# Rationing the clock-keeping matmuls of TensorE by an account kept over all steps instead of one per step

## The chip, the cores and the metric

The kernel runs on one core of one Trainium2 chip. The metric is the device time of one execution in microseconds (us), as the median of several runs. "Clock" is the share of TensorE's clock that the profile says was granted. Each timed run lists its mean clock. From it I work out the **half-clock time** of a run as 2 x (1 - clock) x span, since the clock rows of these traces hold only two values, 1.0 and 0.5. It includes the end of a run, of which up to 2.5 us are at half clock in these profiles.

## The reference

```python
def reference(A_x, A_wqkv, A_wo, B_u, ..., gate_w):      # cut to what matters
    x = A_x                                              # 2048 x 512, bf16
    g = sigmoid((x * gate_w).sum(-1, keepdims=True))
    a = attention(x, wqkv, wo)        # 32 heads of 16: softmax(q k^T / 4) v, then @ wo
    b = ssm_conv(x, A, B, C, dt, D)   # S4 layer: a convolution over the sequence, plus x * Dskip
    return g * a + (1 - g) * b
```

The attention has 32 x 2048 x 2048 scores, and each needs an exponential. The rest (the S4 layer, the projections, the gate) is background work that has to fit in beside them.

## The kernel before

The kernel is written by a scheduler in Python. It goes through 683 *steps*. In each, ScalarE takes the exponential of one tile of scores (up to 128 x 1536 elements, two such tiles in PSUM, `SC0` and `SC1`). While it does, TensorE makes the scores of the tile after the next ("fill": three matmuls with 32 rows each, side by side: in the trace the three start within 7 ns and the group takes 0.39 us), multiplies earlier exponentials with V ("P·V", into `OA`: groups of four matmuls with 32 columns each, side by side, 0.40 us for a group) and runs background matmuls into `MB`. From the middle on, VectorE makes the exponential of the third slice of some tiles, so that ScalarE has 1024 columns in those steps instead of 1536.

TensorE has time left in most steps. It is filled with **zero matmuls** (`keep`, weights `wm`, which hold zeros). They compute nothing; they are there to keep the clock up (where more of them were put into starved steps, half-clock time fell from 27 to 8 us and from 62 to 28 us: "Block ends" below). They go into `OA` while a block of P·V is open there (adding zero), else into `OA` once its transpose on VectorE is scheduled, else into `MB` if it is free. An account called `units` decides how many: each step starts at 0, a fill counts 1, four P·V matmuls count 1, a background matmul its `u`, a zero matmul 1, and zero matmuls are added up to 3.2.

```python
    def keep(b, clear=False):
        o = MB if b is None and not clear else OA
        return mm(lambda: o(0, [[1, 512]]), lambda: wm(0, [[1, P]]), lambda: wm(0, [[0, 4], [1, 128]]), [(wm, 0)],
                  [(o, 0, "warm" if b is None else b)], b is None, b is None, c=.24)
    ...
    while tile(t + 1):                     # one step
        t += 1
        p.put(ex(t))                       # the exponential of tile t
        e0 = p.aend                        # its end, and that of the next one, by the scheduler's clock
        e1 = e0 + (512 * len(acols(t + 1)) / 1200 + EXP if tile(t + 1) else 0)
        sch.units = 0.0
        ...
            put(*fill(t + 2))
            sch.units += 1
        ...
        lim = e1 + .25
        pvs(t, lim)                        # P·V
        sch.run(e0, lim, e1)               # background work
        pvs(t, lim)
        while sch.units < 3.2 and p.free["PE"] + .3 < lim:
            if opened:                                       # a block of P·V is open in OA
                o = keep((pvn - 1) // 16)
            elif f"t{(pvn - 1) // 16}" in sch.flag and pvn < NQ:   # OA's transpose is scheduled
                o = keep(None, True)
            elif sch.lock.get("MB") is None:
                o = keep(None)
            else:
                break
            if p.ready([o]) is None or p.ready([o]) > p.free["PE"] + .05:
                break
            put(o)
            sch.units += 1
```

Background matmuls carry `u` per matmul: 0.125 for `Qt`·`X` (eight per bank), about 0.03 for `Tt`·`X` and `Py`·`SG`, 0.05 for the gate's one-column matmuls, 1 for the projections.

The softmax here doesn't subtract the row's maximum and nothing guards it: scores larger than these inputs give would overflow.

## Time and profile before

| | before |
|---|---|
| time, median of the first three runs | 915.44 us (915.36, 915.44, 920.25) |
| span of the profiled run | 919.1 us |
| ScalarE busy | 882.7 us, 96% |
| TensorE busy | 846.4 us, 92%, with 832 zero matmuls |
| half-clock time in the profile, before the kernel's end | 75 us in ten stretches |
| gaps over 60 ns before an exponential | 19.7 us |

From the page of the kernel before (PE is TensorE's matmuls, PEld its weight loads, DVE VectorE, ACT ScalarE, POOL GpSimd, SP SyncE; L570 is the line of a helper that writes all matmuls): busy time of engines with share of the span, then some rows of the 40 equal slices (busy tenths; `PEclk` is the granted clock in tenths), the chain of work that ended last by engine, and three groups of instructions (line, engine, operation, out<-in, count | busy us, mean ns | idle before it and what ended it).

```profile
PE 846.4 (92%) x7684; PEld 265.0 (29%) x7684; DVE 808.5 (88%) x1684; ACT 882.7 (96%) x693; POOL 10.3 (1%) x18
...
PE   8999989888898888998899999989899999999997
...
ACT  6999999999999999998998999998999999999996
...
PEclk9999989999999989997997998897999999999999
...
ACT 39%; PE 37%; DVE 19%; issue 2%; SPq 1%; POOL 1%; DMA 0%; DVEq 0%; POOLq 0%; ACTq 0%
...
L723 ACT ACTIVATE ET<-SC 128x1536 bf16<-128x1536 f32 x322 | 435.8, 1608 | 8.7 <-PE SC L570 8.4
L723 ACT ACTIVATE EL<-SC 128x1536 bf16<-128x1536 f32 (+1 forms) x343 | 415.7, 1357 | 11.7 <-PE SC L570 9.5
...
L570 PE MATMUL OA<-wm 128*128 128x512 bf16 x827 | 262.2, 403 | 1.0 <-DVE wm L629 1.0
```

ScalarE is the engine to win time on, and it is already 96% busy. TensorE looks as full, but almost a third of its busy time, 262 us, is zero matmuls. The `PEclk` row has dents, at slices 6, 15, 19, 22, 25, 26 and 28. The windows view puts numbers to them: length of the stretch, busy us of PE, PEld, DVE, ACT and POOL in it (number of instructions), then granted clock, share of DMA time and GB/s. The first stretch is an undisturbed one.

```profile
100.00:120.00 20.00, 19.75 (x134) 5.58 (x132) 18.56 (x27) 19.98 (x16) 0.00 (x0) 1.00 0.00 1
420.00:440.00 20.00, 17.97 (x144) 4.65 (x143) 17.61 (x35) 17.36 (x14) 0.00 (x0) 0.74 0.26 73
560.00:580.00 20.00, 18.21 (x281) 7.29 (x277) 17.30 (x51) 18.39 (x14) 0.00 (x0) 0.74 0.68 167
620.00:640.00 20.00, 20.00 (x261) 7.00 (x255) 16.63 (x49) 17.14 (x14) 0.00 (x0) 0.74 0.66 157
```

At a mean clock of 0.74 ScalarE is busy for 17.1 to 18.4 us of 20 instead of 19.98. The timeline of TensorE inside such a stretch shows why (start us, length us, engine, line, operation, out<-in, shape, how many in a row, idle time before it):

```profile
430.07 0.61 PE L570 MATMUL SC<-Qm,KT 32*128 32x512 bf16 x3
430.61 0.62 PE L570 MATMUL OA<-ET,VE 128*32 128x512 bf16 x4
431.15 0.65 PE L570 MATMUL MB<-Qt,X 64*32 64x256 bf16 x8
431.74 0.61 PE L570 MATMUL OA<-wm 128*128 128x512 bf16 x1
432.28 0.61 PE L570 MATMUL SC<-Qm,KT 32*128 32x512 bf16 x3
```

And ScalarE in the same stretch:

```profile
430.73 1.45 ACT L723 ACTIVATE ET<-SC 128x1536 bf16<-128x1536 f32 x1 [0.60 <-PE SC L570]
432.93 1.45 ACT L723 ACTIVATE ET<-SC 128x1536 bf16<-128x1536 f32 x1 [0.76 <-PE SC L570]
```

From fill to fill this step takes 2.21 us; an undisturbed one takes 1.34. Zero matmuls in a row start 0.40 to 0.43 us apart in the half-clock stretches of this trace and 0.22 to 0.23 us apart at full clock. The scores come late, and the exponential at 432.93 has waited 0.76 us for them.

Just ahead of another fall of the clock (at 163.41 us) TensorE looks like this:

```profile
160.23 0.39 PE L570 MATMUL SC<-Qm,KT 32*128 32x512 bf16 x3
160.55 0.40 PE L570 MATMUL OA<-ET,VE 128*32 128x512 bf16 x4
161.57 0.39 PE L570 MATMUL SC<-Qm,KT 32*128 32x512 bf16 x3 [0.62 <-ACT ET L723]
162.91 0.39 PE L570 MATMUL SC<-Qm,KT 32*128 32x512 bf16 x3 [0.95 <-ACT ET L723]
```

This is a block end: the last P·V of a block is at 160.55, `OA` then waits for its transpose on VectorE, and two steps get no zero matmul at all. TensorE idles 0.62 and 0.95 us, and at 163.41 us the clock is halved.

In the kernel before, the clock rows between the first and the last one (20) are whole multiples of 3.413 us long: those at half clock 3.41, 6.83, 10.24 or 13.65 us. So the clock changes on a grid of that step. In this document a *window* is one step of that grid, and the window before a fall is the step that ends where the clock falls.

### The profile page before, as it was taken

Reading aid. Unit: us, or ns where it says so; the run is one execution under the profiler, and the core shown is the slowest. Engines: PE = TensorE matmul, PEld = TensorE weight load, DVE = VectorE, ACT = ScalarE, POOL = GpSimd, SP = SyncE. Lnnn points to the kernel's source line nnn. Section 1 sums busy time; section 2 is a strip of 40 time slices with the busy share of each in tenths; the row PEclk is TensorE's granted clock in tenths of the full one; section 3 lists DMA queues with packets and bytes.
Section 4 is the critical chain, followed back from the end, with each engine's and each line's share of the span. In section 5 each row is a group of like instructions: output and inputs, shape, how many; then the busy total and the mean of one; then the engine's idle time right before and its main releaser. Section 6 shows DMA issues by size and latency. Waiting matters only on the chain.

```text
span 919.1 us, 18539 instructions
## 1 busy us (share of the span) xinstructions
PE 846.4 (92%) x7684; PEld 265.0 (29%) x7684; DVE 808.5 (88%) x1684; ACT 882.7 (96%) x693; POOL 10.3 (1%) x18
## 2 busy tenths in 40 slices
PE   8999989888898888998899999989899999999997
PEld 3222222222222222222223433323334323222222
DVE  7999899997479999998998999898989898899972
ACT  6999999999999999998998999998999999999996
POOL 2000000000000000000000000000000000000000
PEclk9999989999999989997997998897999999999999
DMA  8350000007779666964827496826624100000000
GB/s 200 93 92 1 1 1 1 1 1 207 224 214 249 174 199 181 208 168 106 228 60 175 108 167 172 163 54 142 136 63 116 25 30 25 6 1 1 1 2 23
DMA packets 227411, 92.30 MB, mean 100 GB/s; under 512 B 191872, under 2 KB 215040, under 8 KB 225280
## 3 DMA queue, kind: packets, MB, share of 16 engines
q1 hardware_dynamic: 226128, 90.34, 40.3%
q8 instruction: 60, 0.98, 0.4%
q10 hardware_dynamic: 1200, 0.79, 0.3%
q14 instruction: 23, 0.19, 0.1%
HBM read 27.92 MB, written 35.65 MB: 69 GB/s over the span
## 4 chain that ended last, share of the span: by engine, by line
ACT 39%; PE 37%; DVE 19%; issue 2%; SPq 1%; POOL 1%; DMA 0%; DVEq 0%; POOLq 0%; ACTq 0%
ACT ET L723 21%; PE OA L570 20%; ACT EL L723 16%; PE SC L570 11%; PE MB L570 6%; ACT EX L723 3%; DVE tt L835 3%; DVE Sst L1062 2%; DVE G L1112 2%; DVE s L1110 2%; DVE s L1108 2%; DVE s L1106 2%; DVE SG L1114 1%; DVE PT L835 1%; SPq L1024 1%
## 5 line engine op out<-in xcount | busy, mean ns | idle before, releaser
L723 ACT ACTIVATE ET<-SC 128x1536 bf16<-128x1536 f32 x322 | 435.8, 1608 | 8.7 <-PE SC L570 8.4
L723 ACT ACTIVATE EL<-SC 128x1536 bf16<-128x1536 f32 (+1 forms) x343 | 415.7, 1357 | 11.7 <-PE SC L570 9.5
L570 PE MATMUL SC<-Qm,KT 32*128 32x512 bf16 x2048 | 274.8, 396 | 48.3 <-ACT ET L723 21.1
L570 PE MATMUL OA<-wm 128*128 128x512 bf16 x827 | 262.2, 403 | 1.0 <-DVE wm L629 1.0
L570 PEld LDWEIGHTS SC<-Qm,KT 32*128 32x128 bf16 x2048 | 66.8, 91 | 315.7 <-ACT ET L723 130.4
L570 PE MATMUL OA<-EL,VE 128*32 128x512 bf16 x1028 | 112.9, 401 | 1.3 <-DVE OT L824 1.3
L734 DVE TENSOR_SCALAR EL<-SC 128x512 int16<-128x512 f32 x122 | 82.9, 681 | 22.3 <-PE SC L570 21.6
L570 PE MATMUL OA<-ET,VE 128*32 128x512 bf16 x966 | 99.4, 406 | 0.1
L570 PEld LDWEIGHTS OA<-wm 128*128 128x128 bf16 x827 | 56.7, 99 | 110.7 <-issue 95.7
L835 DVE TENSOR_TENSOR tt<-B,D 128x1024 bf16<-128x1024 bf16 x96 | 62.6, 680 | 0.5
L1062 DVE TENSOR_TENSOR Sst<-MB,sgn 128x512 bf16<-128x512 f32 x64 | 43.6, 682 | 13.4 <-PE MB L570 13.2
L1112 DVE TENSOR_TENSOR G<-s,s 128x256 f32<-128x256 f32 x120 | 50.8, 423 | 3.5
L1106 DVE TENSOR_TENSOR s<-G,MU 128x256 f32<-128x256 f32 x120 | 49.8, 415 | 0.1
L1108 DVE TENSOR_TENSOR s<-G,MU 128x256 f32<-128x256 f32 x120 | 49.9, 416 | 0.0
L1110 DVE TENSOR_TENSOR s<-s,SG 128x256 f32<-128x256 f32 x120 | 49.8, 415 | 0.0
L570 PE MATMUL OA<-DC,VC 128*32 128x512 bf16 x122 | 46.3, 379 | 0.0
L570 PE MATMUL OA<-DP,VE 128*32 128x512 bf16 x122 | 46.2, 379 | 0.0
L824 DVE STREAM_TRANSPOSE OT<-OA 128x512 f32<-128x512 f32 x32 | 22.7, 711 | 26.1 <-PE OA L570 26.0
L570 PEld LDWEIGHTS OA<-EL,VE 128*32 128x32 bf16 x1028 | 29.7, 94 | 54.2 <-issue 46.2
L835 DVE TENSOR_TENSOR DC<-DC,DP 128x1024 bf16<-128x1024 bf16 x61 | 41.9, 686 | 1.0
L835 DVE TENSOR_TENSOR DC<-EL,DP 128x1024 bf16<-128x1024 bf16 x61 | 41.7, 684 | 1.0
L570 PEld LDWEIGHTS OA<-ET,VE 128*32 128x32 bf16 x966 | 24.6, 94 | 56.4 <-issue 52.9
(148 smaller groups left out, 715.2 us busy)
## 6 DMA issues: line engine op xcount, KB each, us to landing
gm_ptd<-PT SPq DMA_DIRECT2D x16, 1024.0 KB, 6.0
Py<-gm_ptd SPq DMA_DIRECT2D x32, 512.0 KB, 4.7
gm_sd<-Sst SPq DMA_DIRECT2D x64, 128.0 KB, 2.0
gm_kpd<-Kst SPq DMA_DIRECT2D x16, 256.0 KB, 3.1
Tt<-gm_kpd SPq DMA_DIRECT2D x128, 32.0 KB, 3.6
gm_xrd<-in_A_x_dram SPq DMA_DIRECT2D x1, 2048.0 KB, 11.0
X<-gm_xrd SPq DMA_DIRECT2D x8, 256.0 KB, 4.8
gm_ytd<-Yst SPq DMA_DIRECT2D x32, 64.0 KB, 2.3
```

The source lines that it names most:

```text
L570: return O("PE", lambda t: t.matmul(out(), lhsT(), rhs(), start=start, stop=stop, skip_group_check=True, **kw), R, W, c, l, u)
L723: return ac(lambda a: a.activation(b(o, F), sc(0, F), AF.Exp, scale=LN2 / 128), [(sc, n, (t, n)) for n in ns], [et(t, n)[2] for n in ns], ...
L734: yield [dv(lambda v: v.tensor_scalar(b(o, [[1, 512]]).bitcast(I16), sc(512 * n, [[1, 512]]), -EOFF, EOFF, ALU.max, ALU.add), [(sc, n, (t, ...
L824: yield [dv(lambda v: v.transpose(OT(0, [[1, 512]]), OA(0, [[1, 512]])), [(OA, 0, b)], [(OT, 0, b)], 560)]
L835: return dv(lambda v: v.tensor_tensor(o(), a(), b_(), f), R, W, n, k)
L1024: yield [dma("SP", lambda e: e.dma_start_transpose(Qt((blk % 2) * PTN, [[128, 32], [1, 128]]), ptd.dram(blk * P * PTN, [[PTN, P], [1, PTN] ...
L1062: yield [dv(lambda v, bank=bank: v.tensor_tensor(Sst(512 * bank, [[256, 2], [1, 256]]), MB(0, [[256, 2], [1, 256]]), sgn(0, [[0, 2], [1, 2 ...
L1106: yield [dv(lambda v: v.tensor_tensor(s2(0, V2), G(0, V2), MU(d0, [[0, 2], [1, 128]]), ALU.mult), key("G", "MU"), [(s2, 0)], 256)]
L1108: yield [dv(lambda v: v.tensor_tensor(s3(0, V2), G(128, [[-128, 2], [1, 128]]), MU(D + d0, [[D, 2], [1, 128]]), ALU.mult), key("G", "MU") ...
L1110: yield [dv(lambda v, so=so: v.tensor_tensor(s2(0, V2), s2(0, V2), sg(so, [[RS, 2], [1, 128]]), ALU.add), [(s2, 0)] + ks, [(s2, 0)], 256)]
L1112: yield [dv(lambda v: v.tensor_tensor(G(0, F), s2(0, F), s3(0, F), ALU.add), [(s2, 0), (s3, 0)], [(G, 0)], 256)]
L1114: yield [dv(lambda v, so=so: v.tensor_copy(sg(so, [[RS, 2], [1, 128]]), G(0, V2)), key("G"), last, 256, 2)]
```

## The change

The account is kept over all steps. What one step could not deliver is owed (`debt`, at most 4) and asked of the next; a surplus is not credited. The rate is 2.2 per us of ScalarE time instead of 3.2 per step, and a fill counts 0.75, its share of the array (3 x 32 of 128 rows). While more than 2.5 is owed, background matmuls that bring little on this account for their time ("thin": gate, `Qt`·`X`, `Tt`·`X`/`Py`·`SG`) are held back.

```diff
+WARM = 2.2
+DEBT = 2.5
@@ Sched
-        self.n, self.units = 0, 0.0
+        self.n, self.units, self.debt = 0, 0.0, 0.0
@@ Sched.run, for a background matmul
-                    if max(f, r) + c > pe_end:
+                    if max(f, r) + c > pe_end or self.debt - self.units > DEBT and sum(o.u for o in ops) < 2.3 * c:
                         continue
@@ fill
-                         pos=(32 * j, 0), c=.325 / len(sl), l=.4, u=1 / len(sl)))
+                         pos=(32 * j, 0), c=.325 / len(sl), l=.4, u=.25))
@@ the step
+        sch.debt = max(0.0, min(4.0, sch.debt - sch.units)) + WARM * (e1 - e0)
         sch.units = 0.0
...
-            sch.units += 1
+            sch.units += .75
...
-        while sch.units < 3.2 and p.free["PE"] + .3 < lim:
+        while sch.debt - sch.units > .2 and p.free["PE"] + .3 < lim:
```

## The prediction

> **What bounds the kernel now.** ScalarE: the page gives ACT 882.7 of 919.1 us (96%), nearly all the 683 exponentials of L723. TensorE reads 92%, but 832 of its matmuls are zero matmuls that only keep its clock up. So the change can win only what ScalarE idles inside the loop. The gaps over 60 ns before an exponential add up to 19.7 us, about 16 us of it in or just behind ten stretches at half clock: 132.7-139.5, 163-167, 221-225, 327-334, 399-402, 426-436, 457-464, 491-501, 570-583 and 621-631 us, some 75 us together (clock row of the page; the windows view by 20 us shows clock 0.74 and ACT 17.1 to 18.4 at the worst). There a step takes about 2.06 us in place of 1.34: scores, P·V and zero matmuls follow each other at half rate and the next exponential waits for the scores.
>
> **Why the clock falls.** [...] halved stretches last 3.41, 6.83, 10.24 or 13.65 us. Counting array share times columns (a 128x128x512 matmul = 1), windows before a fall hold 3.3 to 6.0, normal ones 7 to 12. Two things make low windows: block ends, where OA is being transposed and MB locked, so neither P·V nor zero matmuls go (160.2-162.9); and thin matmuls that the account overrates (a bank of Qt·X counts 1.0, is 0.50; eight gate matmuls count 0.4, are 0.016).
>
> **What the change does.** The old account asks 3.2 per step, fill as 1; the new 2.2 x 1.343 = 2.95, fill as 0.75. A normal step gets the same zero matmuls: two with a P·V, three without. New: (1) a shortfall is carried (up to 4), so a starved step is followed by up to four; (2) gate, Qt·X and Tt·X/Py·SG matmuls wait while over 2.5 is owed; (3) steps of 1024 columns are asked about 2.0 and get one zero matmul fewer. Replaying the account by hand over the trace's steps changes their number hardly: some 10 more before 480 us, 30 fewer after 640 us; some 25 thin groups are held. A zero matmul is about 0.22 us of TensorE (timeline).
>
> **On the critical path.** Windows that fall on a starved pair of steps alone still drop the clock. What goes are falls where starvation and thin work meet (gate at 124-132, Qt·X at 324-328 and 423-427, y units at 487-500, 564-580, 617-628), and stays at half clock are shorter. I take 40% of the 16 us: 6 us; the last stage gains perhaps 0.5. Against it: extra matmuls at half clock delay scores, DVE's 122 exponentials may change by a few (each saves 0.43 us of ScalarE: 1450 against 1020 ns), and new falls may appear.
>
> Predicted: 909 us, range 900 to 917. Faster by over 2%: 0.04; within 2%: 0.93; slower by over 2%: 0.03. Even with every fall gone, 915.4 - 16 = 899 is 1.8%.
>
> **What shows it right.** Half-clock time from 75 to 40-50 us, fewer falls after 480 us; ACT busy unchanged within 3 us; zero matmuls 780 to 840; DVE exponentials 118 to 126.
>
> **What would make it wrong.** [...] If block-end starvation alone causes them, nothing changes. If DVE exponentials fall by over 10, or deferred thin work holds MB and delays projections, it gets slower.

Its sum is 915.4 - 6 - 0.5 = 909. Its windows are the 3.413 us steps of the clock rows. A second count of that trace by array share gives 3.2 to 5.9 in the windows before the ten falls and 4.75 to 15 in the other full-clock ones (the middle 80%: 6.75 to 11.25), where it says 3.3 to 6.0 and 7 to 12. That low windows cause the falls was its estimate; the count over all traces is below.

## The result

| | before | after |
|---|---|---|
| median | 915.40 us (913.95 to 920.25, 4 runs) | 904.08 us (903.59 to 904.24, 4 runs) |
| span of the profiled run | 919.1 us | 902.2 us |
| half-clock time in the profile | 75 us, ten falls | 20.5 us, four falls |
| gaps over 60 ns before an exponential | 19.7 us | 7.2 us |
| ScalarE busy | 882.7 us | 878.4 us |
| zero matmuls | 832 | 855 |
| VectorE exponentials | 122 | 122 |

The ratio is 0.9866 (95% interval 0.983 to 0.9903). It is the mean time of the fast runs of the changed kernel over that of the fast runs of the kernel before, of the same rounds, so it is not quite the ratio of the medians. It is 1.3% faster, clear of noise.

The same lines of the page of the changed kernel:

```profile
PE 827.8 (92%) x7687; PEld 265.4 (29%) x7707; DVE 805.4 (89%) x1684; ACT 878.4 (97%) x693; POOL 10.3 (1%) x18
...
PE   7999989888899889888889999999999999999997
...
ACT  6999999999999999999999999999999999999996
...
PEclk9999999999999899999999999999999999999999
...
ACT 62%; PE 26%; DVE 10%; issue 1%; POOL 1%; ACTq 0%; DVEq 0%; POOLq 0%
...
L725 ACT ACTIVATE ET<-SC 128x1536 bf16<-128x1536 f32 x322 | 434.6, 1726 | 4.3 <-PE SC L572 4.2
L725 ACT ACTIVATE EL<-SC 128x1536 bf16<-128x1536 f32 (+1 forms) x343 | 412.7, 1388 | 3.4 <-PE SC L572 1.8
...
L572 PE MATMUL OA<-wm 128*128 128x512 bf16 x849 | 259.6, 392 | 1.0 <-DVE wm L631 1.0
```

The dents in the clock row are gone but for one digit. The chain that ended last now runs 62% through ScalarE where it was 39%: where it left ScalarE for TensorE and VectorE before, it now stays. The waits view names what went: the first two lines are of the kernel before (waiting instruction <- what it waited for: total us, times, longest).

```profile
ACT EL L723 <- PE SC L570: 9.5, 24, 0.7
ACT ET L723 <- PE SC L570: 8.4, 17, 0.8
```

The changed kernel:

```profile
ACT ET L725 <- PE SC L572: 4.2, 7, 0.9
ACT EL L725 <- PE SC L572: 1.8, 6, 0.5
```

The windows view of the changed kernel in the stretches that were worst (the work in them is not exactly the same, as it runs up to 17 us earlier):

```profile
420.00:440.00 20.00, 15.71 (x151) 5.04 (x147) 19.93 (x40) 19.25 (x15) 2.12 (x1) 1.00 0.52 115
560.00:580.00 20.00, 18.56 (x278) 7.79 (x278) 19.38 (x60) 20.00 (x16) 0.00 (x0) 1.00 0.58 137
620.00:640.00 20.00, 18.93 (x320) 8.62 (x316) 19.40 (x58) 20.00 (x16) 0.00 (x0) 1.00 0.58 131
```

The 16.9 us between the two spans add up. Gaps before exponentials fell by 12.5 us. ScalarE's busy time fell by 4.3 us, of which I estimate 4.0 from the trace: there are 59 such gaps before and 23 after, and an exponential behind a gap lasts 1.45 instead of 1.34 us (36 x 0.11). The start and the tail around the exponentials are the same (14.4 and 8.9 us in both). The profiled run of the kernel before is among its slowest, 920.9 us (33 runs reach 920.96), which is why the spans differ by more than the medians.

All four falls that are left in the changed kernel stand behind a block end. Two of them, at 483.31 and 589.12 us, have only scores, P·V and zero matmuls in the window before; the other two, at 131.73 and 305.81 us, have also thin work there, gate and `Qt`·`X`. This one is at 483.31 us:

```profile
480.42 0.40 PE L572 MATMUL OA<-EL,VE 128*32 128x512 bf16 x4
481.44 0.39 PE L572 MATMUL SC<-Qm,KT 32*128 32x512 bf16 x3 [0.62 <-ACT EL L725]
482.79 0.39 PE L572 MATMUL SC<-Qm,KT 32*128 32x512 bf16 x3 [0.95 <-ACT EL L725]
483.11 0.90 PE L572 MATMUL OA<-EL,VE 128*32 128x512 bf16 x8
483.94 1.03 PE L572 MATMUL OA<-wm 128*128 128x512 bf16 x2
```

The shortfall is repaid, but only from 483.11 us on, and the window before the fall ends at 483.31.

### The profile page after: what moved, and what is told of

It is laid out like the page before. It is cut to its first block, busy times and chain, and to the rows that moved or that the text cites. A ratio compares the mean times of both kernels' runs of the same rounds, so it can differ in the third digit from the quotient of the medians.

```text
span 902.2 us, 18566 instructions
## 1 busy us (share of the span) xinstructions
PE 827.8 (92%) x7687; PEld 265.4 (29%) x7707; DVE 805.4 (89%) x1684; ACT 878.4 (97%) x693; POOL 10.3 (1%) x18
## 4 chain that ended last, share of the span: by engine, by line
ACT 62%; PE 26%; DVE 10%; issue 1%; POOL 1%; ACTq 0%; DVEq 0%; POOLq 0%
ACT ET L725 33%; ACT EL L725 26%; PE OA L572 14%; PE SC L572 8%; PE MB L572 5%; ACT EX L725 3%; DVE tt L837 1%; DVE Sst L1064 1%; DVE G L1114 1%; DVE s L1112 1%; DVE PT L837 1%; DVE s L1108 1%; DVE s L1110 1%; DVE SG L1116 0%; DVE EL L736 0%
## 5 line engine op out<-in xcount | busy, mean ns | idle before, releaser
L572 PE MATMUL SC<-Qm,KT 32*128 32x512 bf16 x2048 | 269.4, 388 | 44.3 <-ACT ET L725 19.9
L572 PE MATMUL OA<-wm 128*128 128x512 bf16 x849 | 259.6, 392 | 1.0 <-DVE wm L631 1.0
L572 PE MATMUL OA<-EL,VE 128*32 128x512 bf16 x1028 | 111.0, 391 | 0.1
L572 PE MATMUL OA<-ET,VE 128*32 128x512 bf16 x966 | 96.8, 395 | 0.9 <-DVE OT L826 0.9
L736 DVE TENSOR_SCALAR EL<-SC 128x512 int16<-128x512 f32 x122 | 82.9, 681 | 13.1 <-PE SC L572 12.3
```

The source lines that it names most:

```text
L572: return O("PE", lambda t: t.matmul(out(), lhsT(), rhs(), start=start, stop=stop, skip_group_check=True, **kw), R, W, c, l, u)
L736: yield [dv(lambda v: v.tensor_scalar(b(o, [[1, 512]]).bitcast(I16), sc(512 * n, [[1, 512]]), -EOFF, EOFF, ALU.max, ALU.add), [(sc, n, (t, ...
```

## The experiments

The theory was: the account over steps removes half-clock time, because it repays shortfalls and keeps thin matmuls off the starved steps. Rivals: the new level alone does it; only one of carrying and rationing does it; or it is chance, since any edit makes the scheduler write another order and moves the low windows about. All kernels below gave correct results. "Half-clock" is the mean over the timed runs of each.

| kernel | median us | runs | half-clock us | ratio to before (95%) |
|---|---|---|---|---|
| before (runs with a listed clock) | mean 915.6 (907.88 to 920.96) | 33 | 62 | |
| changed | 904.08 | 4 | 27 | 0.9866 (0.983 to 0.9903) |
| level only | 910.15 | 4 | 57 | 0.9955 (0.9913 to 0.9997) |
| carried, no rationing | 908.62 | 4 | 44 | 0.9942 (0.9888 to 0.9995) |
| before, LAT 0.060 | 907.67 | 4 | 42 | 0.9935 (0.9893 to 0.9978) |
| changed, LAT 0.060 | 902.16 | 4 | 28 | 0.987 (0.983 to 0.991) |
| before, LAT 0.050 | 909.68 | 4 | 53 | 0.9933 (0.9867 to 0.9999) |
| changed, LAT 0.050 | 903.38 | 4 | 26 | 0.9865 (0.98 to 0.993) |
| changed, zero matmuls into scores | 904.54 | 4 | 8 | 0.9911 (0.9824 to 0.9997) |
| before, zero matmuls into scores | 917.62 | 4 | 28 | 1.0033 (0.9961 to 1.0105) |
| changed, into scores only with slack | 908.33 | 4 | 27 | 0.9917 (0.9857 to 0.9977) |
| changed, narrow zero matmuls | 900.34 | 1 | 25 | one look |
| narrow, into scores only with slack | 903.45 | 4 | 21 | 0.9866 (0.9804 to 0.9929) |
| changed, LAT 0.060, narrow | 900.08 | 6 | 27 | 0.9823 (0.9792 to 0.9855) |

Taking each kernel's runs about that kernel's own mean (84 runs in all), one us of half-clock time goes with 0.28 us of kernel time, and that line explains 82% of their variance. So the runs of one kernel differ mostly with their half-clock time.

### The level alone

```diff
-        sch.debt = max(0.0, min(4.0, sch.debt - sch.units)) + WARM * (e1 - e0)
+        sch.debt = max(0.0, min(0.0, sch.debt - sch.units)) + WARM * (e1 - e0)
```

> The changed kernel with the carried shortfall set to zero (clamp 0 in place of 4), so only the new level (2.2 per us, fill as 0.75) is left; the scheduler then never owes over 2.5, so the rationing of thin matmuls never acts either, and it writes 790 zero matmuls in the loop (before 818, changed 841). Theory 'the account carried over steps and what hangs on it makes the gain': 912 to 918 us, half-clock time 60 us or more. Rival 'the new level alone makes it': about 904 us, half-clock about 20 us.

It measured 910.15 us and 57 us of half-clock time. The level does not make the falls go away, so the rival is out, as far as one order can show it. Both numbers are a little below what was expected (912 and 60), at nearly the half-clock time of the kernel before. In the profile the gaps outside half-clock stretches are 1.8 us instead of 4.4 and VectorE makes 124 exponentials instead of 122; as the next pairs show, an order can be worth that much, so I give the level no credit for it.

### Carrying without rationing

```diff
-DEBT = 2.5
+DEBT = 1e9
```

> The changed kernel with the limit DEBT out of reach, so shortfalls are carried and repaid but thin matmuls are never held back (822 zero matmuls). Theory 'holding thin matmuls back while work is owed makes the gain': 911 to 917 us, half-clock time 50 us or more. Rival 'repaying the shortfall makes it': 903 to 907 us, half-clock 20 to 30 us.

It measured 908.62 us with 44 us, between the two expectations. Its four runs are 904.79, 906.95, 910.29 and 914.18. Half-clock time fell by 18 us against the kernel before and has 17 more to go. So neither half of the change is shown to do it alone. But this is one order of each, and the next section shows that orders of one kernel can differ by 20 us of half-clock time. How the gain divides between repaying and holding back stays open.

### Chance: the same kernels in other orders

`LAT` is the latency that the scheduler assumes for a semaphore. Changing it a little says nothing about the account but reshuffles the whole order.

```diff
-LAT = .055
+LAT = .060        # and .050 in the second pair
```

> The kernel before with one unrelated number of the scheduler's model changed (LAT 0.055 to 0.060), which reshuffles the whole order. Rival 'chance: any reshuffle moves the low windows about': anywhere from 900 to 920 us. Theory 'the old account makes the falls': 911 to 920 us, half-clock 60 us or more.

> The changed kernel with the same unrelated number changed (LAT 0.060). Chance: anywhere from 900 to 920 us, no order against the other reshuffled kernel. Theory 'the account makes the gain': 902 to 908 us, half-clock under 35 us, at least 7 us below the reshuffled kernel before.

> The kernel before once more reshuffled by an unrelated number (LAT 0.050). After the first pair (before 915, reshuffled 908; changed 904, reshuffled 902) part of the gain looks like chance. Theory 'the account is worth some 30 us of half-clock time whatever the order': half-clock 40 to 70 us, 907 to 918 us. Chance alone: may be as low as 902 us with under 30 us.

> The changed kernel reshuffled by the same number (LAT 0.050). Theory of the account: half-clock 15 to 35 us, 901 to 907 us, at least 5 us below the kernel before with that number. Chance alone: may be as high as 912 us.

The kernel before measured 907.67 and 909.68 us in the two other orders, so the first expectation (911 or more, half-clock 60 or more) missed for it: the order of the original kernel is an unlucky one. The changed kernel measured 902.16 and 903.38 us, both in the ranges expected; but the first pair is 5.5 us apart where at least 7 was expected, the second 6.3. Over three orders each, the means are 915.6, 908.5 and 909.8 for the old account and 904.0, 902.5 and 903.6 for the new one: 911.3 against 903.4 us on average, 7.9 us. Half-clock time is 62, 42, 53 against 27, 28, 26. The mean of every order of the new account lies below that of every order of the old, which three against three would do by chance once in 20 times; the half-clock times, apart in the same way, support it. I take the account as real and worth about 8 us, and the other 3 to 4 us of the measured difference as the luck of the order before. The half-clock difference, 25 us at 0.28, would explain 7.

### What the windows before a fall hold

The new account weighs a matmul by its share of the array. I counted each trace in windows of 3.413 us, laid on the grid of its own clock rows, by two measures, both my own. *Array share*: rows x columns of the weights / 128² (a wide zero matmul has 128x128, the largest in these traces) x moving columns / 512. *Time*: the time in which at least one matmul streams, which I estimate from its start as 0.216 us per 512 moving columns (zero matmuls in a row start 0.215 to 0.228 us apart at full clock), so that matmuls side by side count once. The two give nearly the same for wide zero matmuls. They part when the zero matmuls are made narrow, with nothing else changed:

```diff
-        return mm(lambda: o(0, [[1, 512]]), lambda: wm(0, [[1, P]]), ...
+        return mm(lambda: o(0, [[1, 512]], 0, 32), lambda: wm(0, [[1, 32]]), ...
```

> The changed kernel with every zero matmul in the loop narrowed to 32 output columns of the array (weights 128x32 in place of 128x128; same moving size, same number, same order, same time on TensorE). Theory 'what counts for the clock is the share of the array in use': a zero matmul counts a quarter, windows fall under the mark almost everywhere, half-clock time over 400 us and the kernel over 1000 us. Rival 'what counts is the time in which TensorE is busy': within 10 us of 904 us, half-clock under 40 us.

It measured 900.34 us in one look, with 25 us of half-clock time. The theory of the array's share, mine and the account's, falls. The count of windows says it as clearly. In the eleven kernels with wide zero matmuls, 42 of the 52 full-clock windows under 5 by array share were followed by a fall (a matmul counts where it starts); in the three kernels with narrow ones only 13 of 117 were. By time the same limits part both kinds in these traces. All 45 full-clock windows in which TensorE streams for under 1.3 us of the 3.41 were followed by a fall, 34 of the 41 between 1.3 and 1.5 us, and none of the 3394 (734 of them with narrow ones) at 1.5 us or more. That is all 79 falls of these traces. In the trace of the kernel before, leaving out the fall at the end of a run here, the windows before its ten falls hold 0.90 to 1.44 us of streaming and every other full-clock window 1.55 or more. In that of the changed kernel the four before a fall hold 1.06, 1.09, 1.37 and 1.49 us, and every other one 1.51 or more, but for one at the start (12.3 us: 1.39, with one missing matmul record put in from its weight load) that no fall followed. The falls go with the columns streamed and not with the time that a group takes: eleven of the falls have 16 to 32 gate matmuls of one column in the window, and if these counted at the 0.21 us that eight of them take, all eleven windows would be over 1.5 us.

### Block ends

If starved block ends make the falls that are left, a zero matmul needs a place that is always free. The scores of the next tile but one are such a place: right behind the fill, adding zero to them. (The edit sends a zero matmul there whenever the one of `OA` and `MB` that the loop picked is not ready. By a print added to the scheduler, it counted `MB` as free for 36 of the 62 zero matmuls that went into the scores, so the edit is wider than the expectation says.)

```diff
+    def keep_sc(t):
+        sc = SC[t % 2]
+        return mm(lambda: sc(0, [[1, 512]]), lambda: wm(0, [[1, P]]), lambda: wm(0, [[0, 4], [1, 128]]), [(wm, 0)],
+                  [(sc, 0, (t + 2, 0))], False, True, c=.24)
...
             else:
-                break
-            if p.ready([o]) is None or p.ready([o]) > p.free["PE"] + .05:
-                break
+                o = None
+            if o is None or p.ready([o]) is None or p.ready([o]) > p.free["PE"] + .05:
+                if not tile(t + 2):
+                    break
+                o = keep_sc(t)
```

> The changed kernel, in which a zero matmul that finds neither OA nor MB free goes into the scores of the next tile but one, adding zero to them; nothing else. All four falls left in the changed kernel follow a block end with two steps without zero matmuls. Theory 'those starved pairs cause the falls that are left': 896 zero matmuls, half-clock time under 14 us in the profile, 897 to 902 us. Rival 'the falls have another cause, or the extra matmuls delay the scores': 903 us or more.

> The kernel before with the same extra place for zero matmuls and its old account per step (908 zero matmuls). Theory 'starved pairs at block ends cause most falls': half-clock under 35 us, 901 to 908 us. If instead the overrated thin matmuls cause most: half-clock 45 us or more, 909 us or more.

The cause of most falls is confirmed, in one order of each kernel, and the cure fails. Half-clock time fell to 8 us (3.4 us and one fall in the profile), which the mean of no other kernel here comes near. The time stayed at 904.54 us, where 897 to 902 was expected. In the kernel before half-clock time fell from 62 to 28 us, and the time did not fall with it: 917.62 us, where 901 to 908 was expected; its profile has 16.9 us of gaps, only 5.2 of them in or behind half-clock stretches. TensorE of the changed kernel with this edit:

```profile
449.10 0.39 PE L572 MATMUL SC<-Qm,KT 32*128 32x512 bf16 x3
449.42 0.40 PE L572 MATMUL OA<-ET,VE 128*32 128x512 bf16 x4
449.76 0.61 PE L572 MATMUL SC<-wm 128*128 128x512 bf16 x2
```

And ScalarE:

```profile
450.40 1.45 ACT L725 ACTIVATE ET<-SC 128x1536 bf16<-128x1536 f32 x1 [0.47 <-PE SC L572]
```

The scores are filled at 449.10 and would be there by 449.49. The two zero matmuls behind P·V write to the same bank until 450.37, and the exponential, which could have begun at 449.93, begins at 450.40. The profile has 8.8 us of gaps before exponentials, as against 7.2 in the changed kernel, and only 2.4 of them lie in or behind the half-clock stretch. A warm clock was bought with late scores. So I allowed the zero matmul only in steps without P·V and with 0.65 us to spare:

```diff
-                if not tile(t + 2):
+                if not tile(t + 2) or pvn > pv0 or p.free["PE"] + .65 > e1:
```

> As the kernel with zero matmuls in the scores, but only in a step that issues no P.V, and only where 0.65 us are left before the next exponential by the scheduler's clock. The first try cut the half-clock time to about 8 us and still took 904.5 us, with exponentials waiting 0.2 to 0.5 us at full clock at block ends because a zero matmul stood between P.V and their scores. Theory 'that wait ate the gain': half-clock 8 to 18 us, gaps outside half-clock under 3 us, 898 to 902 us. Rival 'half-clock time is no longer worth anything here': 903 us or more.

> The same with every zero matmul of the loop narrowed to 32 output columns. The one look at narrow zero matmuls gave 900.3 us at the usual half-clock time, which says that busy time counts and not the array's share. Theory 'busy time counts': half-clock time as the wide one's within 8 us and the same time within 3 us. Theory 'array share counts': half-clock over 400 us, over 1000 us.

This failed. The wide version is at 908.33 us and its half-clock time is back at 27 us, as in the changed kernel; in its profile 3.5 us of gaps lie outside the half-clock stretches (10.0 in all, 6.5 in or behind them). With so few places left, it removes no falls. Why it is 4 us slower than the changed kernel at the same half-clock time, I have not shown; another order is enough for that much. The narrow version has half-clock time within 8 us, as the theory of time said, but is 5 us faster rather than within 3.

### Narrow zero matmuls as an improvement

Three comparisons of narrow against wide point the same way. The timelines show a reason. With wide zero matmuls (changed kernel; `PEld` is a weight load):

```profile
250.91 0.40 PE L572 MATMUL OA<-ET,VE 128*32 128x512 bf16 x4
251.23 0.33 PEld L572 LDWEIGHTS OA<-wm 128*128 128x128 bf16 x3 [0.23 <-issue]
251.24 0.82 PE L572 MATMUL OA<-wm 128*128 128x512 bf16 x3
```

With narrow ones:

```profile
251.38 0.40 PE L572 MATMUL OA<-ET,VE 128*32 128x512 bf16 x4
251.39 0.31 PEld L572 LDWEIGHTS OA<-wm 128*32 128x32 bf16 x2
251.60 0.59 PE L572 MATMUL OA<-wm 128*32 128x512 bf16 x2
```

The narrow weights are loaded while P·V still runs, 0.01 us behind its start, and the zero matmul starts 0.22 us behind P·V instead of 0.33. The width alone is not the reason: behind another zero matmul the wide weights, too, are loaded 0.01 us behind its start (median of 444 loads in the changed kernel). What goes with the wait is the change from 128x32 weights to 128x128 (0.32 us behind the start of P·V, median of 182 loads there). The last run puts this on the best order seen, as the version to beat both:

> The changed kernel in the order of LAT 0.060 (wide zero matmuls: mean 902.5 us, half-clock about 28 us), with narrow zero matmuls (32 output columns), same number, same order. In the two looks at narrow ones the wait of the weight load before OA matmuls fell from 195 to 145 us, for the narrow weights load while P.V still runs (zero matmul 0.22 us behind P.V, wide 0.33). Theory 'busy time keeps the clock and the narrow ones leave TensorE more slack': half-clock 15 to 35 us, 897 to 901 us. If narrow ones only were lucky: 901 to 906 us. If array share counted: over 1000 us.

It measured 900.08 us (896.45 to 903.10, six runs), ratio 0.9823 (0.9792 to 0.9855) to the kernel before, with 27 us of half-clock time, as good as the 28 us of the wide one. The wide kernel in the same order has 902.16 us and 0.987. The wait of weight loads for `OA` matmuls that no other engine explains, from the waits view of the wide one and then the narrow one:

```profile
PEld OA L572 <- issue: 185.4, 797, 0.4
PE SC L572 <- ACT ET L725: 25.6, 73, 1.0
PE SC L572 <- ACT EL L725: 10.6, 26, 1.2
```

```profile
PEld OA L572 <- issue: 144.6, 627, 0.8
PE SC L572 <- ACT ET L725: 41.3, 151, 1.0
PE SC L572 <- ACT EL L725: 18.2, 61, 1.1
```

41 us less of it. The waits of score matmuls for ScalarE, which is TensorE's slack, rose from 25.6 and 10.6 to 41.3 and 18.2 us. The gain of 2 to 3 us over the wide one is inside what orders and runs differ by, if taken alone; the two intervals against the kernel before overlap. With the other two pairs (904.08 to 900.34 in one look, 908.33 to 903.45) I take it as likely, not as shown.

## Why the prediction was right

The time was predicted at 909 us with a range of 900 to 917, and is 904.08. The gain forecast was 6.5 us and the measured one is 11.3, part of it luck. The chain held: ScalarE idles at half clock; the new account removes part of those stretches; VectorE's exponentials do not change (122 in both). Point by point:

- **What bounds it, and the ceiling.** Right. Of the 12.5 us of gaps that went, 11.3 lay in or just behind half-clock stretches, and the span's 16.9 us add up from gaps and ScalarE's busy time. The ceiling of 16 us was too low by what it left out: an exponential behind a gap is about 0.11 us longer, which gave an estimated 4 us more.
- **"I take 40% of the 16 us: 6 us; the last stage gains perhaps 0.5."** The size was too small for this kernel: 11.3 us by the medians. Half-clock time fell to 20.5 us in the profile and 27 on average, where I had expected 40 to 50; but I had started from the 75 us of one slow run, and from mean to mean it fell by 35 us, at the top of the 25 to 35 forecast. Over three orders each the account is worth 7.9 us, close to the 6.5; the rest is that the order of the kernel before was unlucky, which its runs alone could not tell.
- **"Fewer falls after 480 us".** Right: three falls with 34 us became two with 6.8.
- **"Two things make low windows": block ends, and "thin matmuls that the account overrates".** The first was right, by the run that filled the block ends, but not for the reason given, "MB locked": `MB` is free in the pair of steps that it names (160.2 to 162.9), and the loop did not try it. The second rests on the array's share, which the narrow zero matmuls refute (25 us of half-clock time against 27). By columns streamed a bank of `Qt`·`X` is 1, as the old account had it: its eight matmuls of 256 columns start in two fours, 0.16 us apart. The gate's one-column matmuls were overrated, as I said: eight take 0.21 us of TensorE (128.59 to 128.80 in the trace of the changed kernel), stream eight columns, and by the windows above count no more than these.
- **"Windows that fall on a starved pair of steps alone still drop the clock", and what goes are falls "where starvation and thin work meet".** Half right. Two of the four falls left (483.31 and 589.12) have no thin work in their window. But the gate's fall, which should have gone, stands at 131.73 as long as before (6.8 us), and the falls of the kernel before at 163, 221 and 457 us, which had no thin work in the window, are gone. This is one profile of each kernel, and their grids of 3.413 us lie differently against the first instruction (2.98 and 2.02 us behind it, with whole steps taken off).
- **Indicators.** VectorE exponentials held; ScalarE's busy time moved 4.3 us, not within 3, for the reason above; zero matmuls are 855, above the 780 to 840: matched by step between the two traces there are some 22 more before the step at 480 us, where I had said 10, and some 11 fewer after the one at 640 us, where I had said 30.
- **Runs of one kernel.** The forecast allowed for runs of the kernel before that differ by 5 us. That was too narrow: the original spreads over 13 us in 33 runs, and the order of the schedule matters as well: two other orders of it are 6.5 us faster on average. Why the falls of one kernel differ from run to run, no run here shows.

## What to carry to other kernels

Where filler work keeps a clock up, account for it over all steps, not per step, and repay what a starved step missed. Weigh filler by what the traces show to count, in this case the columns that it streams and not its share of the array: a filler a quarter as wide kept the clock as well here (half-clock time 25 against 27 us, and 27 against 28 us). Look first at why a step gets none (here the loop gave up with a free place at hand), and do not put filler between a result and the engine that waits for it (one exponential here began 0.47 us late for it). Before a gain of one per cent is believed in a kernel written by a scheduler, change an unrelated number of the scheduler in both versions and compare over several orders: here a third of the gain was the luck of one order.
